# Causal attention with a gated linear unit on one core: output blocks across two batches, a second V tile, matmuls that nobody reads, and a new plan

## Chip, core and metric

One core of a Trainium2 chip. The kernel is one program on the five engines: TensorE (PE; its weight loads are shown apart as PEld), VectorE (DVE), ScalarE (ACT), GpSimd (POOL) and SyncE (SP), which here issues all transfers between HBM and SBUF. The metric is device time in microseconds (us) of one execution; several runs are made and their median counts. For one execution there is a profile with every instruction in time.

## What is computed

Eight batches, eight heads of width 64, 576 tokens. Attention with a causal mask and a decay by a running sum, then a gated unit whose gate is a causal convolution over five tokens, and a last projection:

```python
B, H, S, D = q.shape                                   # 8, 8, 576, 64
scores = scale * np.matmul(q, k.transpose(0, 1, 3, 2))
cum = np.cumsum(np.maximum(s, 0.0), axis=-1)
bias = -(cum[:, :, :, None] - cum[:, :, None, :])
scores = np.where(causal, -1000000000.0, scores + np.minimum(bias, 0.0))
attn = softmax(scores)
x = (attn @ v), heads put side by side                 # 8, 576, 512
gate_pre[t] = sum over k of conv_w[k] * x[t - 4 + k]   # 5 taps
gate = sigmoid(gate_pre)
out = (gate * (x @ w_val)) @ w_out                     # 8, 576, 512
```

Inputs and output are float32 in HBM; the matmuls run in bfloat16 and sum in float32.

## The kernel before, in words

**Work units.** A unit `n` is a pair of heads of one batch: `b, p = divmod(n, 4)`, 32 units. The 576 tokens are five blocks of 128, 128, 128, 128 and 64. What is read in a block of 64 is done on a window of 128 (`WIN`, L221: the fifth starts at 448), so that half of it is computed twice.

**One batch.** Q and K are loaded as float32 (`dma_qk`, L513), cast to bfloat16 (`cast_qk`, L517), transposed on PE (`qk_T`, L553) and copied out of PSUM into `QKT` (`qk_evac`, L560). The last 64 tokens go apart (`load_tail`, `tail_T`, `tail_evac`, L521 to L550). V is loaded into the staging tile `vst` (L420): by head pairs for batch 0 (`load_v_pair`, L532), by blocks of tokens for the others (`load_v_block`, L538). Its 65th column is 1, so that the `av` matmul also gives the softmax's sum. `vprime` (L526) multiplies it with the decay `w` into `Vp`, which has two buffers. There is one `vst`: the loads of batch b wait until the four `vprime` of batch b-1 have read it (L716).

**One unit.** Scores in three steps into a pair of PSUM banks (`scores`, L582), exponential on ACT (`exps`, L591, three a unit, 96 in all), causal mask on POOL (`mask`, L596), the products with `Vp` (`av`, L606), the reciprocals and normalisation on DVE (`recip`, `norm`), a transpose on PE (`x_T`, L626), its copy into `xT` (`x_evac`, L633). Then the gate: four taps one after the other (`tap`, L637; on DVE one instruction, on POOL a multiplication and an addition), and `tanh` on ACT (L651).

**After the four units of a batch.** For each of four chunks `c` of 128 columns and each half of the tokens: the value projection on PE (`val`, L655) and the gating on DVE (`glu`, L663) into one of the two `glu` tiles, by the parity of the batch. Then five blocks of tokens: the last projection, four matmuls over `c` with 512 columns each (`outp`, L669), the copy out of PSUM into one of three `ot` tiles (`out_evac`, L674) and the store (`store`, L679). The fifth block computes 128 rows, of which 64 are copied and stored: 40 blocks and 160 matmuls for eight batches.

**The order.** Every step is a task with an engine, an estimate of its duration, a key, tasks that it depends on, and buffers that it takes and gives back (`Plan.add`, L269). `Plan.run` (L279) plays the tasks through: at each moment each engine starts, of the tasks that are ready and whose buffers are free, the one with the lowest key. The eight PSUM banks and the pools `P`, `gp`, `th`, `ot`, `qkf` are handed out there too (L389). The keys are the unit's number plus a value of `DUE` (L226), with other values for the first two and last two batches (`due_of`). `STAY` is a surcharge on a change of matmul kind on PE. `CHOICE` (L246) says for each `x_evac`, tap, `out_evac`, cast and so on which of two or three engines does it. The instructions are then emitted in the order that the play-through gave (L814 to L817), and each engine runs its own in that order; between engines the waits hold. A transfer occupies SP for 0.06 us in the play-through, however many are outstanding (L353).

At the start each of the first casts has a tile of its own (`first`, L693). At the end a check of the reciprocals (L799 to L812) decides between this path and a general one, which is not taken here.

## Time and profile before

| | |
|---|---|
| median of 9 runs | 209.69 us (208.48 to 211.32) |
| the profiled execution | 209.36 us |
| its span, first to last instruction | 207.6 us |
| mean granted clock of TensorE | 0.986 |
| bytes moved | 40.48 MB, 195 GB/s on average |
| stores of `ot` | 32 of 256 KB, 8 of 128 KB, 2.9 and 3.4 us to landing (median) |

The span is what the profile can explain; the rest of the execution's time lies around it. Busy times are sums over the time in which at least one instruction of the engine runs, so that instructions that overlap count once. In the page's lines a group is a source line with its engine, operation and tiles, and then comes its number, its busy time, the mean duration of one, and the idle time before them by what ended it. The page's row of the granted clock is in tenths; `PEclk` is the clock that TensorE was given, which is lower after little work.

### The profile page before, as it was taken

What the parts mean: (1) busy time and instruction counts of PE and PEld (TensorE: products, weight loads), DVE (VectorE), ACT (ScalarE), POOL (GpSimd) and SP (SyncE); (2) the same over time, 40 slices, a digit from 0 to 9 for tenths busy, and PEclk for the clock granted to TensorE, in tenths of its full rate; (3) what the DMA queues carried; (4) which work ended last, traced back from release to release, by engine and by line L of the source; (5) the groups of instructions that cost most, each with busy time, mean ns of one, the idle gap of its engine ahead of it and who ended that gap; (6) DMA issues with size and microseconds to landing.
All of it is one profiled execution on the core that took longest, in us unless ns stands there. A gap on an engine that the chain in (4) does not pass through costs nothing.

```text
span 207.6 us, 6026 instructions
## 1 busy us (share of the span) xinstructions
PE 173.3 (83%) x2411; PEld 118.4 (57%) x2411; DVE 177.3 (85%) x311; ACT 163.3 (79%) x205; POOL 161.3 (78%) x179
## 2 busy tenths in 40 slices
PE   1578786899869997789899899989899999979950
PEld 0346575575647765467674658565576555755620
DVE  3747969999889998589999999999999998999810
ACT  2369878978998999987987997899987998553430
POOL 4184595799959998999399999958975898999300
PEclk9999969999999999999999999999999999999997
DMA  4999999996999799998999731941159120222551
GB/s 136 234 280 290 365 171 212 351 278 159 264 292 340 171 319 233 318 337 190 241 385 274 160 139 25 200 133 54 51 125 232 56 79 0 104 101 79 178 182 62
DMA packets 69230, 40.48 MB, mean 195 GB/s; under 512 B 47109, under 2 KB 63493, under 8 KB 69194
## 3 DMA queue, kind: packets, MB, share of 16 engines
q1 hardware_dynamic: 69194, 40.01, 72.1%
q8 instruction: 21, 0.34, 0.7%
q14 instruction: 15, 0.12, 0.2%
HBM read 30.57 MB, written 9.44 MB: 193 GB/s over the span
## 4 chain that ended last, share of the span: by engine, by line
DVE 24%; ACT 20%; PE 18%; SPq 10%; issue 9%; POOL 8%; DMA 8%; ACTq 0%; DVEq 0%; POOLq 0%
ACT P L592 11%; DVE gp L647 9%; PE banks L672 5%; PE banks L660 5%; DMA out_dram<-ot 4%; DVE xn L623 4%; PE banks L613 4%; ACT QKT L561 4%; SPq L540 3%; DMA qkf<-in_q_dram 3%; ACT th L653 3%; DVE glu L666 3%; DVE gp L649 2%; POOL Vp L528 2%; SPq L534 2%
## 5 line engine op out<-in xcount | busy, mean ns | idle before, releaser
L592 ACT ACTIVATE P<-banks 128x1024 bf16<-128x1024 f32 x96 | 95.0, 1041 | 10.6 <-PE banks L566 8.6
L647 DVE SCALAR_TENSOR_TENSOR gp<-banks,ratio,gp 128x574 f32<-128x574 bf16 (+2 forms) x85 | 67.6, 805 | 2.4 <-POOL gp L645 1.7
L598 POOL TENSOR_SCALAR_AFFINE_SELECT P<-P 128x512 bf16<-128x512 bf16 x64 | 39.4, 637 | 11.4 <-ACT P L592 11.2
L566 PE MATMUL banks<-QKT 64*128 64x128 bf16 (+4 forms) x576 | 37.6, 245 | 9.0 <-ACT P L592 4.9
L660 PE MATMUL banks<-xT,wv 128*128 128x288 bf16 x256 | 40.2, 285 | 3.2 <-DVE glu L666 1.4
L672 PE MATMUL banks<-wo,glu 128*128 128x512 bf16 x160 | 39.6, 379 | 1.4 <-ACT QKT L561 0.8
L528 POOL TENSOR_TENSOR Vp<-vst,w 128x650 bf16<-128x650 f32 x29 | 37.6, 1314 | 1.3 <-PE banks L546 1.1
L613 PE MATMUL banks<-Vp,P 128*128 128x65 bf16 x960 | 36.1, 196 | 1.3 <-ACT P L592 1.2
L613 PEld LDWEIGHTS <-P 128*128 128x128 bf16 x960 | 34.3, 99 | 5.0 <-issue 2.1
L566 PEld LDWEIGHTS <-QKT 64*128 64x128 bf16 x576 | 19.6, 96 | 26.2 <-issue 19.7
L660 PEld LDWEIGHTS <-wv 128*128 128x128 bf16 x256 | 22.5, 97 | 14.2 <-issue 6.9
L653 ACT ACTIVATE th<-gp,halfw 128x576 f32<-128x576 f32 x32 | 25.2, 793 | 6.2 <-POOL gp L645 3.4
L561 ACT COPY QKT<-banks 128x1024 bf16<-128x1024 bf16 x25 | 25.5, 1047 | 3.7 <-PE banks L557 3.6
L666 DVE SCALAR_TENSOR_TENSOR glu<-th,banks 128x288 bf16<-128x288 f32 x64 | 27.9, 445 | 0.5 <-PE banks L660 0.3
L623 DVE TENSOR_TENSOR xn<-banks,recs 128x640 bf16<-128x640 f32 x32 | 26.2, 819 | 0.3
L677 ACT COPY ot<-banks 128x512 f32<-128x512 f32 (+1 forms) x26 | 15.3, 588 | 11.3 <-PE banks L672 6.9
L672 PEld LDWEIGHTS <-glu 128*128 128x128 bf16 x160 | 14.6, 97 | 15.5 <-issue 2.7
L649 DVE SCALAR_TENSOR_TENSOR gp<-xT,ratio,banks 128x576 f32<-128x576 bf16 x25 | 20.2, 809 | 1.6 <-ACT xT L635 0.9
L644 POOL TENSOR_TENSOR tmp<-xT,ratio 128x576 f32<-128x576 bf16 (+3 forms) x18 | 20.6, 1142 | 0.6 <-DVE xT L635 0.2
L645 POOL TENSOR_TENSOR gp<-tmp,gp 128x573 f32<-128x573 f32 (+2 forms) x11 | 15.7, 1430 | 3.1 <-DVE gp L647 2.3
L631 PE MATMUL banks<-ident,xn 128*128 128x128 bf16 x160 | 14.1, 219 | 3.0 <-DVE glu L666 1.1
L557 PE MATMUL banks<-ident,qb 128*128 128x128 bf16 x128 | 13.5, 233 | 2.4 <-ACT qb L518 1.4
(63 smaller groups left out, 169.7 us busy)
## 6 DMA issues: line engine op xcount, KB each, us to landing
out_dram<-ot SPq DMA_DIRECT2D x32, 256.0 KB, 2.9
qkf<-in_q_dram SPq DMA_DIRECT2D x7, 1024.0 KB, 8.0
qkf<-in_k_dram SPq DMA_DIRECT2D x7, 1024.0 KB, 10.0
vst<-in_v_dram SPq DMA_DIRECT2D x28, 256.0 KB, 5.9
vst<-in_v_dram SPq DMA_DIRECT2D x15, 128.0 KB, 4.1
first<-in_q_dram SPq DMA_DIRECT2D x4, 256.0 KB, 3.4
first<-in_k_dram SPq DMA_DIRECT2D x4, 256.0 KB, 3.7
tail<-in_q_dram SPq DMA_DIRECT2D x8, 128.0 KB, 8.5
```

The costliest lines, as they stand in the source:

```text
L528: eng.tensor_tensor(Vps[b % 2][:, :, h], vst[:, :, h], w[:, :, b * 8 + 2 * p:b * 8 + 2 * p + 2].unsqueeze(3).to_broadcast([128, NKB, 2, 65 ...
L561: copy[e](QKTs[b % 2][:, :, p, 0:512].rearrange("d w (x j) -> d w x j", j=4), slot["qt", b, p].rearrange("d w (j x) -> d w x j", j=4))
L566: nc.tensor.matmul(ps[:, hh, c0:c0 + nq], QKTs[b % 2][r, 1, p, k0:k0 + 128], QKTs[b % 2][r, 0, p, q0:q0 + nq], **kw)
L592: nc.scalar.activation(out=slot["Pt", n][:, :, step * 512:(step + 1) * 512], in_=slot["s", n, step], func=AF.Exp, scale=0.125)
L598: nc.gpsimd.affine_select(out=d, in_=d, pattern=[[0, 4], [1, 128]], compare_op=ALU.is_ge, fill=0.0, base=0, channel_multiplier=-1)
L613: nc.tensor.matmul(ps[:, hh, qb * 65:qb * 65 + 65], lhsT, Vps[b % 2][:, kb, 2 * p + hh, :], start=(kb == 0), stop=(kb == qb))
L623: nc.vector.tensor_tensor(xns[b % 2][:, :, p * 128:(p + 1) * 128].rearrange("t g (h d) -> t h g d", h=2), pv[:, :, :, 0:64], recs[:, n].un ...
L647: nc.vector.scalar_tensor_tensor(gp[:, o:S], slot["x", n][:, 0:S - o], r, gp[:, o:S], ALU.mult, ALU.add)
L653: nc.scalar.activation(out=th, in_=slot["g", n], func=AF.Tanh, scale=halfw[:, n % 4, :])
L660: nc.tensor.matmul(ps, wv[:, dc, c * 128:(c + 1) * 128], xTs[b % 2][:, dc, 2 + o:290 + o], start=(dc == 0), stop=(dc == 3))
L666: nc.vector.scalar_tensor_tensor(glus[b % 2][:, c, o], slot["t", n][:, o], 1.0, slot["v", n, hf], ALU.add, ALU.mult)
L672: nc.tensor.matmul(ps, glus[b % 2][:, c, WIN[i]:WIN[i] + 128], wo[:, c, :], start=(c == 0), stop=(c == 3))
```

## The change

- **Output blocks across two batches.** The two `glu` tiles become one of 2 x 576 columns. Two batches together are nine full blocks of 128 tokens; an even batch does four of them, an odd one five, the first of which (block 4) is half the even batch's last 64 tokens and half its own first. 36 blocks in place of 40, all of 128 rows. What a later batch overwrites is guarded by `old_o`, now also on `val`.
- **Last projection by chunks.** For the last batch each of the four matmuls of a block is a task of its own, with a key by chunk and block.
- **Two V staging tiles.** `vst` is doubled; V of batch b waits for `vprime` of batch b-2. Before batch 1 uses the second one, five of the first Q and K loads land in it (`vraw[1]`), and its frame of ones and zeros is set afterwards. Batch 1's V comes by head pairs.
- **Unread products.** After the play-through `warm` goes along PE's tasks, and where the plan has PE idle for more than 0.3 us and little busy in the last 3.4 us, it puts matmuls of the identity with itself (128x512) into the free bank that has been free longest. Transposes count 0.4 as work in it. Nobody reads them. It places 54.
- **`ot` has five tiles** in place of three.
- **A new plan.** All values of `DUE`, `STAY` and `CHOICE` are others; the start has keys of its own; the casts of batch 1 and the first tail's cast may choose an engine. The model's durations on POOL are raised (mask 0.60 to 0.635, `vprime` 1.25 to 1.33, a tap 2.25 to 2.5), and SP can run at most 9.7 us ahead of the transfers (`BEHIND`).

```diff
-STAY = (0.1, 54.75)
+STAY = (1.42, 130.04)
+BEHIND = 9.7
+FILL = (0.85, 0.3, 3.4)
...
-              xe="00100010001000010000000000010010",
+              xe="00110000011111000011010000101011",
...
-              oute="1000001110101000010100010100011010000010")
+              oute="0000101000000100010000000100000000011010")
...
                 if e == "SP":
-                    idle_at[e] = now + 0.06
                     dma_free = max(dma_free, now + 1.2) + us
+                    idle_at[e] = max(now + 0.06, dma_free - BEHIND)
...
+def warm(order, filler):
+    used = [[] for _ in range(8)]
+    for t in order:
+        for i in t["banks"]:
+            used[i].append([t["start"], None])
+        for i, at in t["freed"]:
+            used[i][-1][1] = at
+    busy, out, end = [], [], 0.0
+    for t in order:
+        if t["eng"] == "PE":
+            gap = t["start"]
+            while end > 3.0 and gap - end > FILL[1]:
+                load = sum(max(0.0, min(b, end) - max(a, gap - FILL[2])) * k for a, b, k in busy)
+                if load > FILL[0] * FILL[2]:
+                    break
+                best = None
+                for i in range(8):
+                    since = max([b for a, b in used[i] if b is not None and b <= end] or [0.0])
+                    if all(b is not None and b <= end or a >= gap for a, b in used[i]) and (best is None or since < best[0]):
+                        best = (since, i)
+                if best is None or end - best[0] < 0.3:
+                    break
+                out.append(partial(filler, best[1]))
+                busy.append((end, end + 0.22, 1.0))
+                end += 0.22
+            end = t["done"]
+            quiet = any(kind == "bank" and tok[0] in ("qt", "tt", "x") for kind, tok in t["take"])
+            busy.append((gap, end, 0.4 if quiet else 1.0))
+        out.append(t["emit"])
+    return out
...
-    plan = Plan(dict(P=3, gp=2, th=6, ot=3, qkf=3))
+    plan = Plan(dict(P=3, gp=2, th=6, ot=5, qkf=3))
...
+    vraw = [one.tile([128, NKB * 8 * 65], FP32, name=f"vst{j}") for j in range(2)]
+    vsts = [a.rearrange("p (i h d) -> p i h d", i=NKB, h=8) for a in vraw]
+
+    def v_frame(j):
+        nc.gpsimd.memset(vsts[j][:, :, :, 64:65], 1.0)
+        nc.gpsimd.memset(vsts[j][0:64, 4, :, :], 0.0)
...
-    glus = two("glu", [128, 4, S], BF16)
+    glu2 = one.tile([128, 4, 2 * S], BF16, name="glu")
+    glus = [glu2[:, :, 0:S], glu2[:, :, S:]]
...
+    def filler(i):
+        nc.tensor.matmul(banks[:, i, :], ident, ident.unsqueeze(1).to_broadcast([128, 4, 128]), start=True, stop=True)
...
+    def outp(b, i, cs):
+        if cs[0] == 0:
+            slot["o", b, i] = bank(("o", b, i), 128, DM)
+        o = (4 * (b % 2) + i) * 128
+        for c in cs:
+            nc.tensor.matmul(slot["o", b, i], glu2[:, c, o:o + 128], wo[:, c, :], start=(c == 0), stop=(c == 3))
...
     def store(b, i):
-        nc.sync.dma_start(out=out[b, kbo[i]:kbo[i] + kbs[i], :], in_=slot["ot", b, i][128 - kbs[i]:128, :])
+        r = b // 2 * 2 * S + (4 * (b % 2) + i) * 128
+        nc.sync.dma_start(out=outf[r:r + 128, :], in_=slot["ot", b, i])
...
-            ts = [add("SP", 1.45, n0 + due("lv") + i * 0.01, lambda b=b, i=i: load_v_block(b, i),
-                      [T["vp", b - 1, p] for p in range(4)]) for i in range(NKB)]
+            if b == 1:
+                t = add("POOL", 0.7, DUE["vf"], lambda: v_frame(1), [T["cast", 0, i % 2, i // 2] for i in range(5)])
+                ts = [[add("SP", 1.45, DUE["lv1"] + DUE["lv1d"] * p, lambda p=p: load_v_pair(1, p), [t])] for p in range(4)]
+            else:
+                ts = [[add("SP", 1.45, n0 + due("lv") + i * 0.01, lambda b=b, i=i: load_v_block(b, i),
+                           [T["vp", b - 2, p] for p in range(4)]) for i in range(NKB)]] * 4
...
+                if b % 2 and hf == 0:
+                    old_o = [T.get(("out", b - 2, i)) for i in range(3)]
+                elif b % 2:
+                    old_o = [T.get(("out", b - 2, i)) for i in (2, 3, 4)]
+                elif hf == 0:
+                    old_o = [T.get(("out", b - 2, i)) for i in range(3)]
+                else:
+                    old_o = [T.get(("out", b - 2, i)) for i in (2, 3)] + [T.get(("out", b - 1, 0))]
...
+        for i in range(4 + b % 2):
+            own = [(0,), (0,), (0, 1), (1,), (1,)][i]
+            need = lambda c: [T["glu", n0 + c, hf] for hf in own] + ([T["glu", n0 - 4 + c, 1]] if b % 2 and i == 0 else [])
+            if b == B - 1:
+                t = None
+                for c in range(4):
+                    t = add("PE", 0.22, n0 + DUE["ol"] + DUE["old"] * i + DUE["doc"] * c, lambda b=b, i=i, c=c: outp(b, i, (c,)),
+                            need(c) + [t_wo, t or T["xt", n0 + 3], T["val", n0 + 2, 1]], take=[] if c else [("bank", ("o", b, i))])
+                T["out", b, i] = t
...
-        for t in plan.order:
-            t["emit"]()
+        for emit in warm(plan.order, filler):
+            emit()
```

## The prediction, as put on record before the changed kernel ran

> **What bounds the kernel now.** The profiled execution took 209.36 us, of which the span is 207.6: 1.76 us lie around it. The median of the runs shown is 209.69, 0.33 above that execution. I make the sum on the span and add 2.09 at the end.
>
> First the page: busy time of each engine.
>
> ```profile
> PE 173.3 (83%) x2411; PEld 118.4 (57%) x2411; DVE 177.3 (85%) x311; ACT 163.3 (79%) x205; POOL 161.3 (78%) x179
> ```
>
> No engine is alone: the four lie within 16 us. So an operation that is moved from one to another is no gain by itself; what counts is which engine is fullest in each stage, and how much it idles. For that, the busy time by stages (columns: stretch, its length, then PE, PEld, DVE, ACT, POOL busy with instruction counts, granted clock, DMA share, GB/s). The cut at 178.34 is the end of the last `exps` on ACT.
>
> ```profile
> 0.00:20.00 20.00, 11.17 (x122) 7.47 (x123) 11.80 (x22) 11.10 (x16) 9.48 (x27) 1.00 0.87 229
> 20.00:90.00 70.00, 59.34 (x913) 43.15 (x914) 61.23 (x101) 64.11 (x79) 60.52 (x62) 0.98 1.06 270
> 90.00:170.00 80.00, 74.41 (x1114) 50.39 (x1112) 78.59 (x141) 71.09 (x89) 68.79 (x73) 1.00 0.62 165
> 0.00:178.34 178.34, 152.63 (x2261) 106.42 (x2262) 158.93 (x278) 153.81 (x190) 146.44 (x168) 0.99 0.79 207
> 178.34:207.60 29.26, 20.69 (x157) 11.98 (x152) 18.38 (x34) 9.46 (x15) 14.91 (x12) 0.96 0.36 124
> ```
>
> From 90 to 170 us DVE is the bound: 78.59 of 80, or 98.2%. From 20 to 90 ACT is the fullest, at 64.11 of 70 (91.6%), with the DMA engines saturated (share 1.06). After the last `exps` 29.26 us pass in which ACT has 9.46 us of work.
>
> Then the waits of ACT from 20 to 170 us, and the end of its timeline, with PE's (start, length, work, and in brackets the idle time before it and what ended it):
>
> ```profile
> ACT P L592 <- PE banks L566: 7.2, 12, 1.2
> ACT QKT L561 <- PE banks L557: 1.8, 1, 1.8
> ...
> 193.69 2.12 PE L660 MATMUL banks<-xT,wv 128*128 128x288 bf16 x16
> 195.65 4.48 PE L672 MATMUL banks<-wo,glu 128*128 128x512 bf16 x20
> ...
> 199.42 0.59 ACT L677 COPY ot<-banks 128x512 f32<-128x512 f32 x1 [1.26 <-DMA out_dram<-ot]
> 201.72 0.59 ACT L677 COPY ot<-banks 128x512 f32<-128x512 f32 x1 [1.71 <-DMA out_dram<-ot]
> ```
>
> The last eviction stands at 201.72 because a staging tile `ot` was still being stored, though PE had ended at 195.65 + 4.48 = 200.13.
>
> **The ledger of the new plan.** The counts are those of the built instruction order, the durations the means of the groups by shape. DVE: 7 evictions of `ot` in place of 14, at 0.685 each (-4.8); 8 `x_evac` fewer at 0.451 (-3.6); 2 taps fewer at 0.805 (-1.6); the 3 `tail_evac` at 0.42 and the first tail cast gone (-1.7); 1 first cast in place of 3 (-1.1). Together -12.8: 164.5. ACT: 29 evictions for 26 at 0.59 (+1.8), 8 `x_evac` at 0.662 (+5.3), 3 `tail_evac` at 0.603 (+1.8), 3 first casts at 0.639 (+1.9): +10.8 over 17 instructions. Neighbours on ACT overlap: count times mean gives 182.2 for all 205, busy is 163.3, so 0.09 each; +10.8 - 17 x 0.09 = +9.2: 172.5. POOL: 2 taps more, each 1.14 + 1.42 (+5.1), a second V frame of 0.16 + 0.52 (+0.7): 167.2. PE: 16 projection matmuls fewer at 39.6 / 160 = 0.248 (-4.0): 169.3, and the fillers.
>
> So the fullest engine is ACT, no longer DVE, and POOL comes close behind it. I follow ACT to its last `exps`.
>
> **The path, step by step.** Of ACT's 172.5, some 9.6 come after its last `exps` (9 evictions, 4 `tanh`, 2 `x_evac` by the order, against 9.46 measured now): 162.9 come before it. Up to 20 us it does 11.1 now and has four of the added instructions in the new order (three casts, a `tail_evac`, 2.2 net): 13.3. From 20 us on 149.6 remain. How dense can ACT do them? In the first 70 us it did 64.11. One wait there is for the clock, below: 1.8, which I fill, so 65.9. The other 83.7 I put at 98.2%, the row of DVE where DVE was the fullest engine: 85.2 us. The last `exps` then ends at 20 + 70 + 85.2 = 175.2, 3.1 earlier than 178.34. Nothing in the trace shows ACT that dense beside a POOL with 5.8 us more; so this is bounded from both sides. The low bound is 98.2% all the way: 149.6 / 0.982 = 152.3, end at 172.3. The high bound is ACT's share now, (153.81 - 11.10) / 158.34 = 90.1%: 166.0, end at 186.0. I stay nearer the dense end, since a fullest engine is the one that others wait for.
>
> The tail: after the last normalisation (182.04) DVE has by the order 3 checks (2.85), 13 `glu` at 0.445, 6 taps at 0.805 and 3 evictions, 15.6 now 14.68; PE 40 projection matmuls for 52, -12 x 0.248 = -3.0. DVE gives the limit: its last but one `glu` can't end before 13.2, four blocks of 0.90 and 0.45 follow on PE: 17.3 after the normalisation, against 18.1 now. I take 0.5 of these 0.8 (bounds 0 and -3.0). With `ot=5` no eviction of the last five blocks waits for a store: last matmul to end of eviction is then some 0.75, not 2.18: -1.4 (bounds 0, if the fifth tile is not free either, and -3.0, both waits shown). Tail 29.26 - 1.9 = 27.4.
>
> Span 175.2 + 27.4 = 202.6; with 2.09, **204.7 us**.
>
> **The parts that I cost at nothing, and their cover.** *Nine blocks per pair of batches*: counted above; 36 stores of 256 KB in place of 32 and 8 of 128 KB, off the path until the tail. Block 4 mixes two batches, so it waits for `glu` of the second one, and the first batch's `glu` columns come free later: `val` of two batches on waits for it, with all that is queued behind on PE. The distance is a whole batch, some 20 us: 0, at most one `val` wait of 0.5 to 0.7 as in the rows `banks L660 <- DVE glu`. *Projection by chunks*: in the built order the last twenty projection matmuls still stand block by block behind the last `val`, as before: 0 by itself. *Two V tiles*: V loads no longer wait for `vprime` of the batch before. That wait is 6.6 us on SP's queue, and what it causes is small: PEld on `Vp` 1.0, POOL's casts on loads 2.3. I take 0 beyond the density above, bounds -3.3 and +1.5 (the first loads of V move behind all of the first Q and K, and `wv`'s conversion already waits 1.5 for its load). Every SP issue behind them (the next casts' loads and the stores) moves with them; with stores in five tiles that is hidden. *The first loads into the second V tile*: its frame and loads must wait for five casts; POOL and SP hold them far ahead of batch 1's `av`.
>
> *Fillers*: 54, of which 40 come before the last `av` of batch 0, in groups of at most 8. The trace has no such matmul; the nearest is L672 with 128x512, 4.48 / 20 = 0.224 at full clock. Where the clock is down, the distance of eight transposes is 0.42 in place of 0.23, 1.8 times: 0.40. From 4 to 36 us PE idles 32 - 22.7 = 9.3. At 0.224 the 40 take 9.0 and fit; at 0.40 they take 16.0 and 6.7 stick out. A filler also waits until the last reader of its bank is done, and all of PE stands behind it. What they can win:
>
> ```profile
> 28.00:30.00 2.00, 2.00 (x34) 2.00 (x32) 0.60 (x1) 1.89 (x2) 1.92 (x3) 0.50 0.94 141
> ...
> 28.57 1.86 PE L613 MATMUL banks<-Vp,P 128*128 128x65 bf16 x30
> ...
> 31.71 1.01 ACT L561 COPY QKT<-banks 128x1024 bf16<-128x1024 bf16 x1 [1.82 <-PE banks L557]
> ```
>
> PE is busy throughout, at half clock: thirty `av` matmuls take 1.86 where warm ones take 1.08, and ACT waits 1.82 for the transposes behind them. That is the 1.8 above. Before 20 us the clock column says 1.00, but four transposes take 0.61 there and 0.39 from 20.25 on; I read that as a slow clock too, and take no gain from it (bounds -1.7, ACT's wait for the first transposes, and +6.7).
>
> Against the fillers speaks the Trainium skill, "TensorE: Matmul & The Clock Gate", Part 1: the gate opens only after a window of about 3.4 us of sustained work, and Part 4 says that transposes don't count as such work. The row agrees on the transposes: the clock fell to 0.50 beside a PE that was all busy. By the page, eight fillers of 0.224 are half a window and leave the first microseconds slow, which would give the time of the second rival below; by the row, where dense `av` groups ended the slow stretch, the sum above stands.
>
> **The rivals.** *ACT and POOL choke each other (slower).* Both are near full: POOL up to its last mask has 167.2 less four taps (10.3), 156.9, against 146.4 now. If ACT keeps the share that it had as the fullest engine from 20 to 90 us, 91.6%, the 149.6 take 163.3: 183.3 + 27.4 + 2.09 = 212.8. It decides from a share below 92.8% on (210.7), and break-even is 93.4%. For it: 7.2 us of ACT's waits are for scores on PE, and POOL's masks wait 9.1 for ACT, so the two already stand in each other's way. Against it: these rows come from a stage where DVE, now relieved by 12.8, or the DMA was full. *Cold fillers.* The first three groups, 18 in number, run at 0.40 on the way to the first scores: 18 x 0.176 = 3.2, 207.9. *Denser still.* 98.2% throughout: 172.3 + 27.4 + 2.09 = 201.8. For it: two V tiles and five `ot` tiles take away waits on transfers that the first 90 us are full of; against it, DMA share is 1.06 there and the bytes to load stay the same.
>
> **How the numbers follow.** Forecast 0.42, denser 0.18, cold fillers 0.12, choke 0.28, of which 0.20 lies past +0.5% and 0.08 between: faster 0.72, same 0.08, slower 0.20. About 0.5% (208.6 to 210.7) is what a measurement of this kernel can tell from no change; its runs spread over 208.48 to 211.32. The range holds the forecast, the cold fillers and most of both outer cases: 199.5 to 212.0; about 0.06 lie under it and 0.11 over it.
>
> **What would show it.** In the profile after: ACT the fullest engine at 171 to 174 us, DVE near 165, POOL near 167; ACT's last `exps` end near 175; a share above 95% on ACT from 90 us on; no wait of ACT for `ot` after the last matmul, and a tail of some 27 us; no stretch at clock 0.50 near 28 us, and PE's fillers near 0.22 each. I am wrong if ACT idles more than 17 us before its last `exps`, if fillers stand in front of scores that ACT waits for, or if DVE remains the bound.

## The result, and the profile after

| | before | after |
|---|---|---|
| median of runs | 209.91 us (31 runs) | 212.73 us (10 runs, 211.9 to 213.26) |
| ratio, 95% interval | | 1.0131 [1.0103, 1.0159] |
| profiled execution, its span | 209.36, 207.6 us | 212.67, 211.0 us |
| mean granted clock | 0.986 | 0.966 |
| end of the last `exps` | 178.34 us | 186.42 us |

The change makes the kernel 1.3% slower, where 204.7 us was forecast. Some executions of any kernel fall into a slower state; the ratios leave these out, the medians do not, and no trace is read of kernel e5 below, whose profiled execution was one of them. From the page after, busy time by engine and the clock in 40 slices:

```profile
PE 179.8 (85%) x2449; PEld 119.3 (57%) x2449; DVE 167.9 (80%) x288; ACT 170.7 (81%) x222; POOL 167.7 (80%) x185
...
PEclk9999999995999699999999999999999999999996
```

The work moved as the ledger had it: ACT 170.7 for 172.5, POOL 167.7 for 167.2, DVE 167.9 for 164.5. What differs is where the engines idle. The stages of the kernel after (columns as in the prediction):

```profile
0.00:20.00 20.00, 13.26 (x125) 7.46 (x125) 7.48 (x15) 12.19 (x18) 10.12 (x27) 1.00 0.86 209
20.00:90.00 70.00, 59.44 (x818) 39.52 (x818) 53.25 (x88) 55.08 (x72) 59.07 (x59) 0.93 0.98 246
90.00:170.00 80.00, 73.76 (x1133) 51.13 (x1134) 75.08 (x130) 78.85 (x101) 75.94 (x79) 1.00 0.69 184
0.00:186.42 186.42, 162.30 (x2314) 108.81 (x2315) 151.56 (x258) 161.21 (x208) 158.72 (x178) 0.97 0.77 200
186.42:211.00 24.58, 17.54 (x137) 10.49 (x135) 16.36 (x31) 9.44 (x16) 9.02 (x7) 0.92 0.36 133
```

From them ACT's idle time up to its last `exps`, each the stretch less ACT's busy time:

| stretch | before | forecast | after |
|---|---|---|---|
| 0 to 20 us | 8.9 | 6.7 | 7.8 |
| 20 to 90 | 5.9 | 4.1 | **14.9** |
| 90 to the last `exps` | 9.7 | 1.5 | 2.5 |
| sum of idle | 24.5 | 12.3 | 25.2 |
| work of ACT up to there | 153.8 | 162.9 | 161.2 |
| the last `exps` ends | 178.3 | 175.2 | 186.4 |

From 90 us on, the change does what was forecast: ACT at 78.85 of 80, 98.6% (97.4% of the whole stretch from 90 us to its last `exps`). But the 7.2 us of idle time won there are lost from 20 to 90 us (9.0 more), and the work that ACT took over, 7.4 us, comes on top. Where in that stretch, shows in steps of ten us; first the kernel before, then after:

```profile
40.00:50.00 10.00, 9.85 (x159) 6.75 (x156) 9.93 (x20) 8.01 (x11) 10.00 (x11) 1.00 0.89 232
50.00:60.00 10.00, 8.18 (x113) 5.76 (x113) 8.54 (x13) 9.92 (x13) 8.16 (x8) 1.00 1.15 260
60.00:70.00 10.00, 8.71 (x145) 6.22 (x145) 9.18 (x18) 9.09 (x12) 9.16 (x10) 1.00 1.04 291
70.00:80.00 10.00, 9.35 (x144) 6.52 (x141) 9.81 (x18) 9.93 (x14) 9.32 (x9) 1.00 1.05 265
```

```profile
40.00:50.00 10.00, 4.59 (x47) 2.23 (x47) 4.39 (x7) 6.81 (x9) 8.51 (x11) 0.82 1.07 286
50.00:60.00 10.00, 10.00 (x165) 7.64 (x164) 6.91 (x13) 5.61 (x7) 7.02 (x6) 0.83 1.20 276
60.00:70.00 10.00, 7.81 (x103) 4.86 (x101) 9.82 (x15) 9.44 (x13) 8.98 (x10) 1.00 0.88 218
70.00:80.00 10.00, 9.31 (x142) 6.67 (x142) 7.42 (x16) 6.09 (x8) 9.74 (x10) 0.83 1.14 320
```

Two holes in ACT's column: 40 to 60 us (12.42 of 20 for 17.93) and 70 to 80 (6.09 for 9.93). The first, in the timeline after (start, length, work, idle before it):

```profile
38.95 0.57 SPq L544 DMA_DIRECT2D qkf<-in_moe_w_out_dram  x1
...
45.44 1.47 DVE L463 TENSOR_SCALAR wo<-qkf 128x2048 bf16<-128x2048 f32 x1 [5.41 <-DMA qkf<-in_moe_w_out_dram]
...
49.13 0.61 PE L628 MATMUL banks<-QKT 64*128 64x320 bf16 x4 [2.89 <-DVE glu L728]
...
50.07 2.68 PE L675 MATMUL banks<-Vp,P 128*128 128x65 bf16 x45
```

The last projection's weights `wo` are loaded behind the four V pairs of batch 1 and two tails. The pairs' twelve transfers occupy SP's queue from 23.42 to 37.53, 14.1 us, where the plan lays out 4 x 1.45 = 5.8. DVE stands 5.41 us before the conversion of `wo`, `glu` behind it comes late, PE waits for its bank, its granted clock is 0.50 from 46.5 to 53.3 us, and forty-five `av` take 2.68 us, where thirty take 1.08 at the full clock (the row of the kernel before, below). The second hole, PE's row and ACT's:

```profile
71.84 3.08 PE L722 MATMUL banks<-xT,wv 128*128 128x288 bf16 x16
74.75 2.90 PE L675 MATMUL banks<-Vp,P 128*128 128x65 bf16 x90
...
77.77 1.14 PE L722 MATMUL banks<-xT,wv 128*128 128x288 bf16 x8
78.84 0.78 PE L628 MATMUL banks<-QKT 64*128 64x128 bf16 x12
...
78.02 0.78 ACT L715 ACTIVATE th<-gp,halfw 128x576 f32<-128x576 f32 x1 [3.37 <-POOL gp L707]
79.33 1.94 ACT L654 ACTIVATE P<-banks 128x1024 bf16<-128x1024 f32 x2 [0.54 <-PE banks L628]
```

For 7.0 us, from 71.84 to 78.84, PE does 24 `val`, 90 `av` and a few transposes of earlier units without a score for ACT. The old order alternates; PE before:

```profile
63.05 1.08 PE L613 MATMUL banks<-Vp,P 128*128 128x65 bf16 x30
64.06 0.61 PE L566 MATMUL banks<-QKT 64*128 64x320 bf16 x12
64.61 0.66 PE L660 MATMUL banks<-xT,wv 128*128 128x288 bf16 x4
```

At the end the change wins more than forecast. The last `glu`, the last matmuls and the last eviction after:

```profile
198.29 2.63 DVE L728 SCALAR_TENSOR_TENSOR glu<-th,banks 128x288 bf16<-128x288 f32 x7
...
200.13 4.54 PE L737 MATMUL banks<-wo,glu 128*128 128x512 bf16 x20
204.75 0.58 ACT L741 COPY ot<-banks 128x512 f32<-128x512 f32 x1 [1.14 <-PE banks L737]
```

The wait for `ot` is gone. From the last `exps` to the end 24.58 us pass, for 29.26.

### The profile page after: what moved, and what is told of

Same layout as the page of the kernel before. It is cut to its first block, busy times and chain, and to the rows that moved or that the text cites. A ratio compares the mean times of both kernels' runs of the same rounds, so it can differ in the third digit from the quotient of the medians.

```text
span 211.0 us, 6093 instructions
## 1 busy us (share of the span) xinstructions
PE 179.8 (85%) x2449; PEld 119.3 (57%) x2449; DVE 167.9 (80%) x288; ACT 170.7 (81%) x222; POOL 167.7 (80%) x185
## 3 DMA queue, kind: packets, MB, share of 16 engines
HBM read 30.57 MB, written 9.44 MB: 190 GB/s over the span
## 4 chain that ended last, share of the span: by engine, by line
DVE 26%; ACT 20%; PE 19%; issue 11%; SPq 8%; DMA 8%; POOL 4%; ACTq 0%; DVEq 0%; POOLq 0%
ACT P L654 12%; DVE gp L709 9%; PE banks L675 6%; PE banks L722 5%; PE banks L737 5%; DVE xn L685 4%; DVE glu L728 4%; SPq L596 3%; DVE gp L711 3%; DMA qkf<-in_moe_w_out_dram 3%; DMA vst<-in_k_dram 3%; ACT th L715 2%; SPq L597 2%; ACT QKT L623 2%; DVE xT L697 2%
## 5 line engine op out<-in xcount | busy, mean ns | idle before, releaser
L709 DVE SCALAR_TENSOR_TENSOR gp<-banks,ratio,gp 128x574 f32<-128x574 bf16 (+2 forms) x82 | 65.9, 810 | 3.1 <-POOL gp L707 2.0
L660 POOL TENSOR_SCALAR_AFFINE_SELECT P<-P 128x512 bf16<-128x512 bf16 x64 | 40.5, 653 | 8.8 <-ACT P L654 8.6
L722 PE MATMUL banks<-xT,wv 128*128 128x288 bf16 x256 | 39.2, 291 | 1.0 <-ACT QKT L623 0.4
L737 PE MATMUL banks<-wo,glu 128*128 128x512 bf16 x144 | 35.0, 380 | 0.3
L628 PEld LDWEIGHTS <-QKT 64*128 64x128 bf16 x576 | 18.6, 95 | 26.9 <-issue 19.6
L722 PEld LDWEIGHTS <-wv 128*128 128x128 bf16 x256 | 23.3, 98 | 11.8 <-issue 3.9
L706 POOL TENSOR_TENSOR tmp<-xT,ratio 128x572 f32<-128x572 bf16 (+3 forms) x20 | 23.0, 1149 | 1.2 <-DVE xT L697 0.8
L741 ACT COPY ot<-banks 128x512 f32<-128x512 f32 x29 | 17.2, 606 | 7.3 <-PE banks L737 6.3
L707 POOL TENSOR_TENSOR gp<-tmp,gp 128x572 f32<-128x572 f32 (+2 forms) x14 | 19.9, 1418 | 1.6 <-DVE gp L709 0.5
L737 PEld LDWEIGHTS <-glu 128*128 128x128 bf16 x144 | 12.9, 97 | 14.2 <-issue 1.7
L511 PE MATMUL banks<-ident 128*128 128x512 bf16 x54 | 17.5, 433 | 0.0
```

What stands on the lines that cost most here:

```text
L628: nc.tensor.matmul(ps[:, hh, c0:c0 + nq], QKTs[b % 2][r, 1, p, k0:k0 + 128], QKTs[b % 2][r, 0, p, q0:q0 + nq], **kw)
L660: nc.gpsimd.affine_select(out=d, in_=d, pattern=[[0, 4], [1, 128]], compare_op=ALU.is_ge, fill=0.0, base=0, channel_multiplier=-1)
L709: nc.vector.scalar_tensor_tensor(gp[:, o:S], slot["x", n][:, 0:S - o], r, gp[:, o:S], ALU.mult, ALU.add)
L722: nc.tensor.matmul(ps, wv[:, dc, c * 128:(c + 1) * 128], xTs[b % 2][:, dc, 2 + o:290 + o], start=(dc == 0), stop=(dc == 3))
L737: nc.tensor.matmul(slot["o", b, i], glu2[:, c, o:o + 128], wo[:, c, :], start=(c == 0), stop=(c == 3))
```

## The experiments

The median is that of the kernel's runs, the ratio that to the kernel before on the same chip. The runs were made on several chips, so ratios compare better than medians. For milestones I use the start of some of the 32 normalisations (`norm`, one a unit): they are the same work in all kernels. "ACT 20 to 90" is ACT's busy time in that stretch.

| kernel | median | ratio | 5th norm | 9th | 13th | last | span |
|---|---|---|---|---|---|---|---|
| before | 209.91 | | 43.40 | 64.49 | 88.71 | 181.22 | 207.6 |
| after | 212.73 | 1.0131 [1.0103, 1.0159] | 52.22 | 76.19 | 96.72 | 188.27 | 211.0 |

By this the 3.4 us of the span divide into +8.0 up to the 13th norm, -1.0 from there to the last, and -3.6 behind it.

One profiled execution stands behind each row of milestones, and they are not the same from one execution, or chip, to the next. In the kernels that begin like the kernel after, the first norm lies anywhere from 18.31 (e6) to 20.21 us (e14). Up to the 5th norm the kernel after, e8 and e16 run the same instructions in the same order, as the edits of e8 and e16 come later. Yet the 5th norm comes at 52.22, 50.96 and 47.87 us, behind 5.41, 3.88 and 2.84 us of waiting for `wo`. In e16:

```profile
42.10 1.45 DVE L463 TENSOR_SCALAR wo<-qkf 128x2048 bf16<-128x2048 f32 x1 [2.84 <-DMA qkf<-in_moe_w_out_dram]
...
47.87 0.82 DVE L685 TENSOR_TENSOR xn<-banks,recs 128x640 bf16<-128x640 f32 x1
```

So some 4 us at the 5th norm, or 1 us at another one, are not by themselves the effect of an edit. What several kernels agree on counts for more.

All edits but that of e11 are made to the kernel after; most only move tasks in the finished order, with

```diff
+    def put(t, other, after=1):
+        plan.order.remove(t)
+        plan.order.insert(plan.order.index(other) + after, t)
```

### The wait for `wo`

First theory: the wait of 5.41 us on DVE is the loss. One kernel loads `wo` before the last of the four V pairs in place of behind it (`before` is `put` with the task ahead of the other), one converts it later (behind the last tap of the third unit):

```diff
+    before(T_w["wo"], v1[0])                 # e1
+    put(t_wo, T["tap", 2, 4])                # e2
```

> Only the place of wo's load in SP's order differs from the changed kernel: it stands before the last of batch 1's four V pairs and the two tail loads of batch 2 instead of behind them. In the changed kernel SP issued it at 38.95 us, it landed at 45.4, and VectorE stood 5.41 us before its conversion. Theory A (VectorE's in-order wait for wo is what took the time: it keeps ScalarE's exps of 40 to 60 us back, 12.4 us busy of 20, and lets TensorE go cold): the load is issued near 34.5, lands near 40 to 41, the wait falls to at most 1.5 us, no granted clock of 0.50 in 46 to 54 us, and the median falls from 212.7 by 4 to 8 us, to 205 to 209. Theory B (ScalarE and GpSimd choke each other anyway; the wait only takes up slack that is lost elsewhere): the wait goes, and the time stays within 1 us of 212.7. Theory C (batch 1's V pairs as such are the trouble, because GpSimd stands in order at the scaled V, 34.50 and 39.21, with 0.97 and 0.95 us of wait, and passes masks and the tail cast on late): the last pair comes later still, GpSimd's second wait grows to 2 us or more, and the gain is under 3 us.

> Only VectorE's order differs from the changed kernel: wo's conversion stands behind the last conv tap of head pair 2 of batch 0, five instructions later, so that two glu halves of channel block 3 and three taps don't wait for wo's load. No transfer is moved. Theory A (the five instructions behind the conversion are what the wait of 5.41 us costs: the glu keeps two PSUM banks, TensorE waits 2.89 us for it, goes to a granted clock of 0.50): VectorE's wait moves behind the taps and shrinks to under 2 us, ScalarE is busy 15 us or more of 40 to 60 us against 12.4, and the median falls from 212.7 by 3 to 7 us. Theory B (the time is lost elsewhere anyway): within 1 us of 212.7. Theory C (GpSimd is late because of batch 1's V pairs): VectorE runs through, but TensorE still waits near 45 us for the tail cast on GpSimd (2.14 us in the changed kernel), and the gain is 1 to 4 us, less than that of loading V in blocks.

Measured: 214.07 us, 1.0171 [1.0082, 1.0260], and 212.48 us, 1.0113 [1.0068, 1.0158]. Neither repairs it. In the first (e1), DVE no longer waits for `wo`; its timeline:

```profile
39.21 1.22 DVE L463 TENSOR_SCALAR wo<-qkf 128x2048 bf16<-128x2048 f32 x1
47.68 0.82 DVE L709 SCALAR_TENSOR_TENSOR gp<-banks,ratio,gp 128x574 f32<-128x574 bf16 x1 [7.25 <-POOL gp L707]
```

It waits 7.25 us for a tap on POOL instead, and POOL's last `vprime` waits 5.63 us for V, which `wo` has pushed back. In the second (e2), ACT has 9.71 of 40 to 50 us and the 5th norm comes at 47.77, 4.5 us earlier than in the trace of the kernel after; but e16 has it at 47.87 with the conversion at its old place, so that it is not shown how much of the 4.5 us is the edit's. It is not kept either: the 9th comes at 75.45 and the 13th at 95.98, 0.7 earlier, and ACT has 12.34 of 60 to 80 us, where the kernel after has 9.44 + 6.09 = 15.53. What the first hole gives back, the second one takes.

### How V comes in

Three ways to have V sooner or not at all: batch 1 by five blocks in place of twelve pair transfers; pairs and `vprime` in the order in which the units need them (with the late conversion of e2); V of later batches not loaded.

```diff
+    plan.order[first]["emit"] = lambda: [load_v_block(1, i) for i in range(NKB)]       # e3
...
+    for i, t in enumerate(sorted(v1, key=plan.order.index)):                             # e9
+        t["emit"] = partial(load_v_pair, 1, i)
+    put(T["vp", 1, 0], T["vp", 1, 3])
+    put(T["vp", 1, 1], M["m", 5, 1])
+    put(T["vp", 1, 2], M["m", 6, 1])
+    put(T["vp", 1, 3], T["vp", 1, 2])
...
-                ts = [[add("SP", 1.45, n0 + due("lv") + i * 0.01, lambda b=b, i=i: load_v_block(b, i),
+                ts = [[add("SP", 1.45, n0 + due("lv") + i * 0.01, lambda b=b, i=i: None,   # e10, e15
```

e10 has the late conversion too. e15 also leaves out the pairs of batch 1 and reads batch 0's tile throughout.

> Only the loads of V for batch 1 differ from the changed kernel: five loads of whole row blocks, as in the kernel before, at the place of the first of the four pairs (twelve loads, of which eight of 128 KB and four of 32 KB). In the changed kernel the twelve took SP from 23.42 to 37.53 us, in the kernel before the five took 6.87 us. Theory C, with A (the pairs make everything behind them late, wo's load and the scaled V): SP is through with V near 31 us, wo's load is issued near 32 to 33 and lands near 39.5, VectorE's wait before wo falls below 1 us, GpSimd starts the four scaled V of batch 1 at or before 34.5 and has no second wait, and the median falls from 212.7 by 5 to 9 us, to 204 to 208, the most of the three edits. Theory A alone: the same wait goes, 4 to 8 us. Theory B (the loss comes back elsewhere): within 1 us of 212.7, with the same idle time of ScalarE somewhere before 90 us.

> The late conversion of wo (e2, 212.48 us), and the V of batch 1 in the order in which it is used: the four pairs are loaded 0, 1, 2, 3 instead of 3, 2, 1, 0, and GpSimd scales pair 0 alone before the masks of batch 1, pair 1 behind the masks of head pair 1, pairs 2 and 3 behind those of head pair 2 (in the changed kernel all four stood before the first mask, the one used first last: 34.50 to 40.5). Theory G (the first 80 us are one chain through in-order engines, started by the last V pair of batch 1: load, scaled V, masks, GpSimd tap, VectorE tap, glu, scores, products with V; removing a single wait in it only lets the next in-order neighbour take over, which is why e1 to e8 all have ScalarE busy 44 to 46 us of 20 to 80): the first norm of batch 1 comes near 43 to 45 instead of 47.8 us, the first of batch 2 near 71 to 73 instead of 75.5, and the median falls by 2 to 4 us below e2, to 208.5 to 210.5. Theory H (the loads as a whole set the pace to 80 us): the first norm of batch 1 comes earlier, that of batch 2 stays at 75 to 76, and the median stays within 1 us of 212.5.

> As e2, but V of batches 2 to 7 is not loaded (the scaled V is made from what batches 0 and 1 left in the two staging tiles): 7.1 MB of the 40 MB are left out, some 27 of its issues on SP, no instruction of a compute engine. Theory H (the transfers set the pace to 80 us: their share is 1.06 to 1.27 per slice from 40 to 80 us in e2): the casts of q and k of batches 2 and 3 stop waiting (3.38 us at 60.12 in e2), ScalarE is busy 50 us or more of 20 to 80 against 46.2, and the median falls by 4 to 7 us, to 205.5 to 208.5. Theory G (order, with one late start): ScalarE stays at 45 to 48 us, and the median falls by less than 2 us.

> The changed kernel (212.73 us), its order untouched, without the V loads of batches 1 to 7: every batch scales the V of batch 0. 8.3 MB of 40 and 39 issues on SP are left out, of them the twelve of batch 1 that took SP from 23.42 to 37.53 us; no instruction of a compute engine is. Theory G (the new order is laid out for loads that come earlier than they do; the first late ones, V of batch 1 and wo behind them, shift all that follows): wo's load is issued near 25, VectorE does not wait for it, GpSimd scales V of batch 1 without a wait, the first norm of batch 1 comes at 44 to 48 instead of 52.2, of batch 2 at 69 to 72 instead of 76.2, and the median falls by 4 to 7 us, to 205.7 to 208.7. Theory M (the order would starve ScalarE with all loads in time): ScalarE stays at 44 to 47 us of 20 to 80, and the median falls by less than 2.5 us.

| kernel | median | ratio | 5th norm | 9th | 13th | last | ACT 20 to 90 |
|---|---|---|---|---|---|---|---|
| e3, blocks | 213.52 | 1.0129 [1.0015, 1.0243] | 53.51 | 78.00 | 98.54 | 190.07 | 53.88 |
| e9, order of V | 211.19 | 1.0083 [1.0051, 1.0115] | 46.42 | 74.50 | 95.03 | 186.57 | 56.27 |
| e10, 7.1 MB less | 210.73 | 1.0022 [0.9997, 1.0048] | 49.60 | 74.48 | 95.01 | 186.55 | 56.73 |
| e15, 8.3 MB less | 210.75 | 0.9983 [0.9934, 1.0033] | 50.71 | 75.05 | 95.58 | 187.43 | 56.40 |

Blocks are not faster: `vprime` begins at 38.03 us, after 4.96 us of waiting. The right order of V (with the late conversion) has the 5th norm 5.8 us before that of the kernel after, 1.5 before that of e16, and the 13th 1.7 before that of the kernel after. Without any V load after batch 0 the ratio is 1.5 points lower (on another chip), so the loads have a price. But no work on POOL or DVE waits for V or `wo` in e15 from 20 to 90 us, and ACT still has only 56.40 of the 70 us, 8 short of the old order. With DMA at 0.14 from 70 to 80 us the second hole is there:

```profile
70.00:80.00 10.00, 10.00 (x147) 7.64 (x146) 6.96 (x16) 5.12 (x7) 7.55 (x8) 0.82 0.14 39
```

So late transfers are a part of the loss, and not the larger part of the hole.

### The taps that ACT's `tanh` waits for

In e9 ACT waits 3.44 us for a tap on POOL at 75.65. Five kernels bring forward or move to DVE the last tap of units 4 and 6 (e5 that of unit 4 alone):

```diff
+    put(T["tap", 4, 4], T["cast", 3, 0, 0], 0)                 # e5, e6, on POOL but earlier
+    put(T["tap", 6, 4], T["tap", 6, 3])                        # e6
...
+    for n in (4, 6):                                           # e7, e8, e12: on DVE
+        T["tap", n, 4]["emit"] = partial(tap, "DVE", n, 4)
+        put(T["tap", n, 4], T["tap", n, 3])
```

e5, e6 and e7 have the late conversion; e8 is the taps alone; e12 is e9 and the taps.

> The late conversion of wo (e2, 212.48 us) and one more step: on GpSimd the fourth tap of head pair 0 of batch 1 stands before the cast of batch 3's q instead of behind it. In e2 GpSimd stood 3.38 us at that cast until its load landed (60.12), the tap ended at 64.6, and ScalarE stood 2.81 us at the tanh behind it, with exps queued behind the tanh. Theory E (GpSimd's order: taps whose tanh ScalarE meets in front of exps stand behind casts and scaled V, so each late load passes through GpSimd to ScalarE): the tanh comes near 59 to 60 instead of 64.64, TensorE's wait of 3.60 us at 66.4 goes, and the median falls by 2 to 5 us below e2, to 207.5 to 210.5. Theory F (GpSimd is full from 57 us on, 9.8, 8.4 and 9.8 us of each 10, so what is taken early is paid at the next tanh): the first wait goes, the next one at 76.40 (3.45 us in e2) grows by as much, and the median stays within 1 us of 212.5.

> As e5, and the fourth tap of head pair 2 of batch 1 stands on GpSimd directly behind the first scaled V of batch 2, six instructions earlier (in e2 it ran from 73.69 to 76.4 and ScalarE stood 3.45 us at its tanh). Theory E: both tanh waits go, and the median is 207 or less, 4 to 7 us below e2. Theory F (GpSimd is full): the taps are early, three scaled V and four masks come 2.6 us later, TensorE's products with P and V wait for them, and the median stays within 1.5 us of e5.

> As e2, but the same two taps are done by VectorE, each directly behind the third tap of its head pair: 2 of about 0.81 us there in place of 2 of 2.56 us on GpSimd. Theory E: as e6, 4 to 7 us below e2, 205.5 to 208.5. Theory F (GpSimd's amount of work, not its order): GpSimd gets 5.1 us back where it is full, so this one gains 1.5 us or more over e6, and 4 to 8 us below e2. If neither (ScalarE's loss before 90 us is set by the loads): within 1 us of 212.5, and ScalarE waits for scores whose q and k are not yet cast.

> The changed kernel with the two taps on VectorE as in e7, but wo's conversion at its old place. With e2 and e7 this makes a square of two edits. Theory E with A (two stalls in a row, the first hidden by the second because the order meets again at the second): alone it brings 0 to 4 us, 208.5 to 212.7, less than with the late conversion, and the wait of 5.4 us before wo's conversion stays. Theory A plays no part: the same time as e7 within 1 us.

> e9 and e7 in one: late conversion of wo, V of batch 1 in the order of its use, and the two taps of batch 1 on VectorE (e7 alone: 211.23 us). Theory G: the two gains add, as they are at two places of one chain, 3 to 5 us below e2, to 207.5 to 209.5, which would be level with or below the kernel before. Theory H: 210.5 to 212.5, no more than e7.

| kernel | median | ratio | 5th norm | 9th | 13th | last |
|---|---|---|---|---|---|---|
| e5 | 211.69 | 1.0062 [1.0018, 1.0106] | - | - | - | - |
| e6 | 211.23 | 1.0107 [1.0006, 1.0208] | 48.08 | 74.47 | 95.20 | 186.75 |
| e7 | 211.23 | 1.0070 [1.0023, 1.0118] | 48.16 | 74.39 | 94.93 | 186.46 |
| e8 | 213.11 | 1.0144 [1.0071, 1.0217] | 50.96 | 77.11 | 97.67 | 189.21 |
| e12 | 211.58 | 1.0076 [1.0041, 1.0112] | 46.45 | 74.44 | 94.99 | 186.54 |

In e6, e7 and e12 ACT's wait for POOL's tap is gone, and yet the 9th norm stays between 74.39 and 75.45, as in e2, e9 and e10. ACT now waits for the scores behind PE's row instead, 6.1 us in e6 and 5.1 in e12. PE there:

```profile
69.34 3.82 PE L722 MATMUL banks<-xT,wv 128*128 128x288 bf16 x16 [1.55 <-DVE gp L709]
72.99 2.90 PE L675 MATMUL banks<-Vp,P 128*128 128x65 bf16 x90
...
77.08 0.78 PE L628 MATMUL banks<-QKT 64*128 64x128 bf16 x12
```

The same row as in the kernel after; it starts 2.5 us earlier, its first sixteen `val` take 3.82 at a fallen clock, and the scores come 1.8 earlier.

### Clock and fillers

Fillers left out of the kernel after; put into the kernel before; and thirteen more into e12 between the scores of units 9 and 10, where its clock falls at 66.0 us:

```diff
-        for emit in warm(plan.order, filler):                                   # e4
-            emit()
+        for t in plan.order:
+            t["emit"]()
...
-        for t in plan.order:                                                    # e11, on the kernel before
-            t["emit"]()
+        for emit in warm(plan.order, filler):
+            emit()
...
+    for n, i, times in ((9, 2, 2), (10, 0, 2), (10, 1, 2), (10, 2, 7)):          # e14
+        for _ in range(times):
+            plan.order.insert(plan.order.index(T["s", n, i]) + 1, dict(eng="", banks=(), freed=(), emit=partial(filler, 6)))
```

> The 54 products into free PSUM banks are left out; nothing else differs from the changed kernel. Theory D (the fillers cost more than they bring: ten of them before 12.1 us took 0.43 to 0.47 us each, and the first exps came at 12.62 us against 9.50 before): first exps about 1 us earlier, and the median 0.5 to 2 us below 212.7. The step of the prediction (they are hidden, and their warm clock is worth up to 1.7 us): the first four transposes of q and k from 12.95 us take 0.6 us per four instead of 0.39, and the median is 0 to 2 us above 212.7. Theories A to C: no change over 1 us either way, and VectorE's wait of 5.4 us before wo's conversion stays.

> The kernel before with the fillers alone: the same rule puts 29 products into free PSUM banks at TensorE's planned gaps, 13 of them ahead of the first scores; everything else is the kernel before. The step of the prediction (hidden, at most 1.7 us of gain, at most 6.7 us of loss if all are cold and in the way): ratio 0.992 to 1.005. Theory D (the early, cold ones cost about what the warm ones bring): first exps 0.5 to 2 us later than 9.50 us, ratio 0.997 to 1.008.

> As e12 (211.58 us), and 13 more fillers into the bank that the early taps have freed, between the score steps of head pairs 9 and 10 (62.9 to 69.3 us in e12), where TensorE had 0.4 to 0.6 us of work in each 0.9, went to a granted clock of 0.50 at 66.0 and stayed there until 72.6; its 16 val products took 3.82 us there against 1.98 at full clock, the 90 products with P and V 2.90 against 2.69 at best. Theory K (the cold clock is what is left of the loss between 57 and 75 us): no row below 0.90 from 62 to 76 us, val 2.0 us, the first norm of batch 2 at 72.4 to 73 instead of 74.44, and the median 1.5 to 2.2 us lower, 209.4 to 210.1. Theory L (VectorE's taps and GpSimd hold the next steps anyway): val is short, TensorE waits longer behind it, and the median stays within 0.7 us of 211.6.

Measured: e4 212.24 us, 1.0059 [1.0016, 1.0101], norms 49.01, 76.02, 96.48, 188.03. e11 209.63 us, 0.9977 [0.9939, 1.0014]. e14 212.09 us, 1.0094 [1.0047, 1.0141], norms 47.64, 74.19, 94.72, 186.26. In the profiles the fillers are worth 0.2 us either way at the last norm (188.27 with, 188.03 without; before 181.22 without, 181.42 with); by the ratios, which for the kernel after come from different chips, they cost it up to 0.7%, and nothing in the kernel before.

e14 has the full clock from 20 to 90 us. Its row on PE; ACT's `exps` behind the row, in e12 and then in e14; and ACT's largest waits in e14 from 36 to 90 us (total, times, longest):

```profile
70.79 2.12 PE L722 MATMUL banks<-xT,wv 128*128 128x288 bf16 x16
72.75 2.90 PE L675 MATMUL banks<-Vp,P 128*128 128x65 bf16 x90
...
76.83 0.78 PE L628 MATMUL banks<-QKT 64*128 64x128 bf16 x12
```

```profile
77.66 1.94 ACT L654 ACTIVATE P<-banks 128x1024 bf16<-128x1024 f32 x2 [5.07 <-PE banks L628]
...
77.41 1.94 ACT L654 ACTIVATE P<-banks 128x1024 bf16<-128x1024 f32 x2 [3.65 <-PE banks L628]
```

```profile
ACT th L715 <- DVE gp L709: 4.8, 2, 3.6
ACT P L654 <- PE banks L628: 4.8, 3, 3.7
```

The sixteen `val` take 2.12 for 3.82, but the row starts 1.45 later, and the scores come only 0.25 earlier. That is not the clock's doing: this execution runs 1.2 us behind that of e12 from the first norm on (20.21 for 19.01), long before the first added filler at 66.69, and only the other 0.3 us can be the fillers' own. ACT's wait for these scores falls from 5.07 to 3.65 us, and from the first norm to the 13th e14 takes 74.51 us, e12 75.98, the kernel after 77.45 and the kernel before 69.62. So in the profile the slow clock costs some 1.5 us of that stretch; the ratio shows no gain (1.0094 for 1.0076, on different chips, each 0.4 points or so wide either way). With the waits for `wo` and POOL's last taps and the slow clock gone, and V's down to 0.6, ACT has 57.59 of the 70 us, 2.5 more than after and 6.5 less than before. What it waits for is the order's own: `tanh` for taps on DVE, `exps` for scores.

### One place in PE's order

Scores of unit 11 moved ahead of the row, with all repairs of e12 and alone:

```diff
+    last = M["e", 10, 2]                                                          # e13, e16
+    for t in (M["av", 8, 0], M["av", 8, 1], T["s", 11, 0], M["e", 11, 0], T["s", 11, 1], M["e", 11, 1],
+              *[T[k, n, hf] for n in (4, 5) for hf in (0, 1) for k in ("val", "glu")]):
+        put(t, last)
+        last = t
```

> As e12 (211.58 us; wo's conversion late, V of batch 1 in its order of use, two taps on VectorE), and one step of TensorE's order around 70 us: the 30 products with P and V of head pair 8 and the first two score steps of head pair 11 stand before the 16 val products of batch 1 instead of behind them, behind 60 further products with P and V and 8 more val products; ScalarE's two exps follow. In e12 TensorE worked through that row from 69.34 to 77.1 us, at a granted clock of 0.50 until 72.6, and ScalarE had nothing to do from 70 to 77.6. Theory I (what all of e1 to e12 keep is TensorE's order: the exps come in bursts of three head pairs, because the third must free its P tile through the products with P and V, and these stand in a row with val): the first exps of head pair 11 comes at 69 to 72 us instead of 77.6, ScalarE is busy 48 us or more of 20 to 80 (46.2 in e12), and the median falls by 2 to 5 us, to 206.5 to 209.5. Theory H (something fixed behind it, loads or GpSimd): the exps come earlier, ScalarE then waits as long before the next score step, and the median stays within 1 us of 211.6.

> The changed kernel (212.73 us) with that step of TensorE's order alone. Theory I: it holds without the other edits, as the order meets at this place whatever came before: 2 to 4 us below the changed kernel, 208.7 to 210.7. Theory A (wo's wait decides after all): less than 1 us.

Measured: 213.93 us, 1.0206 [1.0139, 1.0273], and 215.56 us, 1.0302 [1.0227, 1.0378]; worse than without it. ACT in e13:

```profile
73.31 1.94 ACT L654 ACTIVATE P<-banks 128x1024 bf16<-128x1024 f32 x2 [1.70 <-PE banks L628]
75.14 0.78 ACT L715 ACTIVATE th<-gp,halfw 128x576 f32<-128x576 f32 x1
82.43 0.64 ACT L697 COPY xT<-banks 128x576 bf16<-128x576 bf16 x1 [6.51 <-PE banks L693]
```

The `exps` come at 73.31 in place of some 77.6, and then ACT idles 6.51 us, since the row follows. This step pushes the wait on and does not shorten it.

### Another order altogether

The last two kernels keep all of the change but its order: a list of all tasks with engine and bank of each takes the place of the plan's. It was found by shifting single tasks in the written order, in a model with the V pairs' loads at 2.5 to 2.9 us and a slower TensorE after little work. The first loads are in another order too, 39 and 40 instructions go to another engine, and the fillers are placed anew (32 and 43).

```diff
+    plan.order = []                                                               # e17
+    for row in ORDER.split():
+        n, e, start, done = row.split(":")
+        t = plan.tasks[int(n)]
+        if t["pick"]:
+            t["emit"] = partial(t["emit"].func, names[e])
+        t.update(eng=names[e], start=float(start), done=float(done))
+        plan.order.append(t)
...
```

> The changed kernel's tasks, tiles and buffer counts with another order: found by shifting single tasks in the written order, with the loads of V's pairs for batch 1 put at 2.5 to 2.9 us in the planner's table instead of 1.45 (their issues took 14.1 us for four in the changed kernel) and TensorE's work put at nearly twice its length after a stretch of low use. It also takes other PSUM banks, and 39 instructions go to another engine. wo and V pairs 1 and 0 of batch 1 are loaded first, and the fillers are placed anew, 32. Theory O (order is what costs; structure and resources are sound): the 13th norm comes at 88 to 93 us instead of 96.7; with the changed kernel's own 91.55 us from there to the last norm and 22.7 us behind it the span is 202.5 to 207.5, and the median 204.5 to 209.5, at or below the kernel before. Theory P (two batches' blocks, chunks, two V tiles or fillers cost by themselves): no order of them beats the kernel before, the median stays at 211 or more.

> A second order found in the same way from another start (43 fillers, 40 instructions on another engine, GpSimd with 14 us less to do). The same expectations: Theory O 204.5 to 209.5 us, Theory P 211 or more. If the two fall on both sides of the kernel before, the order decides but neither end is the rule.

| kernel | median | ratio | 5th norm | 9th | 13th | last | span |
|---|---|---|---|---|---|---|---|
| 12 | 209.46 | 0.9953 [0.9921, 0.9984] | 46.45 | 71.70 | 91.30 | 183.10 | 207.8 |
| 13 | 208.64 | 0.9878 [0.9837, 0.9918] | 46.78 | 71.35 | 91.46 | 182.68 | 207.2 |

The second ("13") is faster than both kernels: under the one before by 1.2% by the ratio, by 0.7% by the medians on that chip (208.64 and 210.14). Its busy times, its first stages, and the stretch up to its last `exps`:

```profile
PE 179.0 (86%) x2438; PEld 119.1 (57%) x2438; DVE 173.8 (84%) x301; ACT 167.3 (81%) x214; POOL 152.6 (74%) x174
```

```profile
40.00:50.00 10.00, 8.19 (x132) 5.74 (x131) 8.11 (x15) 9.10 (x12) 9.64 (x12) 1.00 1.14 291
...
70.00:80.00 10.00, 9.84 (x164) 7.61 (x162) 9.36 (x20) 5.83 (x7) 8.72 (x8) 0.99 0.96 231
...
20.00:90.00 70.00, 61.30 (x864) 41.46 (x861) 62.89 (x104) 57.42 (x72) 56.12 (x57) 0.95 1.01 256
90.00:170.00 80.00, 75.73 (x1157) 52.46 (x1154) 77.18 (x135) 78.93 (x102) 69.17 (x73) 1.00 0.65 174
...
0.00:180.80 180.80, 161.39 (x2302) 108.58 (x2303) 157.10 (x272) 158.23 (x199) 143.69 (x168) 0.98 0.80 206
```

Against the kernel after, the 13th norm comes 5.3 us earlier, the rest to the last norm is equal (91.22 and 91.55), and behind it 1.8 are lost (24.5 for 22.7). The first hole is gone, and unlike in e2 to e14 its gain is kept (the 9th norm at 71.35). The second is not filled: ACT has 5.83 from 70 to 80. From 20 to 90 us ACT has 57.42 us of work for 55.08, and DVE, which took work over, 62.89 for 53.25. Up to the last `exps`, which ends 5.6 us earlier (180.80 for 186.42), ACT has 158.2 us of work for 161.2 and idles 22.6 for 25.2: so 3.0 of the 5.6 us are work that another engine does, and 2.6 are waits less. In the first ("12"), whose ACT has 60.31 of the 70 us, the last `exps` ends at 181.02, 3.8 us by less work and 1.6 by fewer waits. Order, engines and banks changed together in these kernels; what the order alone brings is open.

## Why the prediction was wrong, point by point

**The step that failed** is in "The path, step by step": "In the first 70 us it did 64.11. One wait there is for the clock, below: 1.8, which I fill, so 65.9." ACT did 55.08. Its last `exps` ended at 186.42 us, past even the high bound of 186.0, which was ACT's old share of 90.1% kept throughout (it had 89.5%), and it idled 25.2 us up to there, where more than 17 was named as a sign of being wrong. Of the 11.2 us by which the last `exps` is later than 175.2, this term makes 10.8; the rest is 1.1 more idle before 20 us and 1.0 more after 90, less 1.7 of work. The 64.11 was a row of the old order, and the change replaces every key of that order. The row of waits beside it was of the same kind: it listed what ACT waited for in an order that would not be there. I took the density over as if it belonged to the stage, and asked nowhere in the sum whether the new order feeds ACT in it.

**What stood in its place.** Shown: the new order leaves ACT idle for 14.9 of these 70 us, mostly at two places; and in every kernel in which single things are taken out, moved or repaired, a wait (e1, e2, e8), the V order (e9), the V loads (e15), one step on PE (e13, e16), the clock (e14, with all of e12), ACT stays at 53 to 57.6 of 70. Two other orders of the same program, with other engines and banks, bring 3.2 and 3.8 us of span back, the second about half of that up to the last `exps` by less work on ACT. Late V and `wo` and the slow clock have a part: together 2.5 of the 10.8 by e14's ACT time, and 2.9 of the 7.8 us by which the way from the first norm to the 13th got longer; e15's ratio puts the loads' price in the whole run at 1.5%. That the rest is the order of the tasks as such is argued, not shown: its share is not isolated from that of the engine choices and the `STAY` surcharge, which the change altered with it.

**ACT as the fullest engine** was right, and so was "the other 83.7 at 98.2%": 78.85 of 80 us is 98.6%.

**The rival that hit the time missed the mechanism.** "ACT and POOL choke each other" gave 212.8 from a share of 91.6% all along. ACT had 78.7% from 20 to 90 us and 98.6% beside a POOL at 75.94 of 80 from 90 to 170, so the two don't choke each other there. Its sum was right by coincidence: its last `exps` was 3.1 us too early (183.3 for 186.4), its tail 2.8 too long.

**The tail** was 24.6 for 27.4: no wait for `ot`, and 22.7 us behind the last norm for 26.4 before. Half of its mechanism held: from the last matmul's end to that of the last eviction 0.66 us pass, 0.75 forecast, 2.18 before. The other half was mis-sized. The sum let the last matmul end 17.3 us after the end of the last norm at the earliest, by DVE's work; it ended 15.6 after it. DVE is full there, as said, but its last `glu` ends 11.8 us after the norm, where the sum had the last but one at 13.2. It counted each instruction at its mean length, though neighbours on DVE overlap as on ACT, where it took that off (the last seven `glu` take 2.63 us, 0.38 each, for 0.445), and the three checks take 2.4 us for 2.85. One more us is won between the last `exps` and the last norm, and 0.4 lost behind the last eviction. The two errors, 11.2 and -2.8, leave a span of 211.0 for 202.6.

**What I costed at nothing.** Fillers: about nothing in the profiles, as said, though not at 0.22 each. Their group on the page and in the trace (count, busy time, mean ns, idle before):

```profile
L511 PE MATMUL banks<-ident 128*128 128x512 bf16 x54 | 17.5, 433 | 0.0
```

The mean of one is 433 ns; it contains overlap with the next one, and seven warm ones in a row take 1.69 us in e14, 0.24 each. The first five took 2.34 us, 0.47 each. The first `exps` came at 12.62 us, 11.23 without fillers and 9.50 before; kernels with the same start as the kernel after lie between 11.67 and 13.56. That is the rival of cold fillers (3.2 of delay), at some 1 us if it is clear of that spread at all, and by the 4th norm nothing of it is left (33.2, and 33.3 without). The fillers do hold the clock: four transposes take 0.40 from 12.95 us on, and 0.62 as late as 18.47 without fillers, where the clock also reads 0.50 from 28 to 30 us. With them that drop is gone, as forecast, and two others came in its place, 46.5 to 53.3 and 70.4 to 73.8 us, behind PE's waits. The row before was read too far when it was said to agree that transposes don't count as work: PE had been busy for only 0.54 to 0.57 of each us from 25 to 28, and partial use explains that fall as well. Two V tiles: no gain that can be told from the rest, and I had not costed that the loads of batch 1, now by pairs and early, stand on SP's queue before `wo`. "Bounds -3.3 and +1.5" named `wv`; the 5.41 us came to `wo`, which my own sentence, "every SP issue behind them moves with them", should have led me to. It cost little by itself in the end (e2, 0.7 us at the 13th norm).

## What to carry to other kernels

The density of an engine in a stage belongs to the order that was profiled; where a change rewrites the order, neither that density nor a list of its waits is a term of the sum, and the feed of the fullest engine must be followed again, work item by work item. A long wait on an in-order engine is priced by what comes next: a milestone some units further on tells whether removing it gains anything, and here 4.5 to 5.8 us at the 5th norm were 0.7 to 1.7 at the 13th. Before a difference at a milestone is put down to an edit, look at two executions of the same instructions: here, on two chips, they were 4.35 us apart at the 5th norm. When single repairs all end at the same milestone, try the whole order anew before repairing further.
